# Attention units that end without TensorE transposes: softmax sums exchanged by transfers

## The chip, the cores and the metric

One Trainium2 chip, one of its cores. The metric is the device time of one execution in microseconds (us), the median of three runs. The kernel is written for one launch, and nothing is computed on the host.

## The reference

The kernel computes one transformer block with a conditioning vector `c`. A row `mod = silu(c) @ w_mod` gives six vectors of 512 (`sa, ca, ga, sb, cb, gb`). Then

```
h = layernorm(x) * (1 + ca) + sa
q, k, v = h @ wq, h @ wk, h @ wv      # 32 heads of 16 columns, one k and one v for all
p = softmax(q k^T / 4)                # 2048 x 2048 for each head
x = x + ga * ((p v, heads side by side) @ wo)
h = layernorm(x) * (1 + cb) + sb
x = x + gb * (relu(h @ w1) @ w2)      # w1: 512 x 1792, w2: 1792 x 512
```

`x` is 2048 x 512, everything is float32.

## The kernel before, in words

**Blocks and units.** The 2048 queries are eight blocks of 256 (`NB`, `TB`). A block has four units, one for each group of eight heads, so there are 32 units (`NU`). A unit holds 8 heads x 256 queries against 2048 keys, in 16 steps of 128 keys (`KT`).

**The main loop** (L837) takes two steps in a turn: 256 turns `c`, eight to a unit. TensorE's 128 x 128 array is used as two halves of 64 rows: a matmul on rows 0 to 63 and one on rows 64 to 127 run side by side, so the program hands out work to the halves in pairs. A turn issues, in the order of the two strings `PARTS` (L39):

- 8 score matmuls (L713, half `h` of each in letters `c` and `d`); ScalarE (ACT) takes the exponential of each into SBUF (L715);
- 8 matmuls for the maxima of the next unit's scores (L417, letters `a` and `b`); VectorE (DVE) reduces each of them (L419). There are three PSUM banks for scores (`ps_exp`) and three for maxima (`ps_max`);
- the products of the exponentials with v, 2 x 4 matmuls on column quarters of the array (L831, `ps_pv`), which end each half of a turn. v carries sixteen columns of ones, so each quarter of `ps_pv` holds 16 rows of sums of p v (numerators) and 16 equal rows of sums of p (denominators), for 2 heads x 256 queries along the free dimension: the quarter's rows 0 to 15 are numerators, its rows 16 to 31 denominators;
- one *portion* of other work, six matmuls or twelve short ones, each issued once for each half (L166, letters `l` and `u`, bank `ps_fill`): first the q projections of later blocks, and from turn 32 on the rest of the layer for the block before (`behind(b)`, L502). Where nothing is left, six dummy matmuls take the portion's place (L855).

**How a unit ends.** `normalise` (L718) copies `ps_pv` to SBUF (ACT, L723). In the next turn, at letter `t`, four 128 x 128 pieces of that copy are transposed on TensorE into a `ps_max` bank, in two halves (`on_half`, L162; a change of half within a bank is fenced by a nop at L159), so that queries lie on the partitions. DVE then takes the reciprocals of the denominators (L731, 128 x 16) and multiplies (L734, twice) into `on[b]`, queries by features.

**What is behind.** `behind(b)` starts at turn 32(b+1) and lasts 32 portions. Before the change these are: 1 portion carried over from block b-1, 4 of the output projection (`out_proj`), 7 of the second layer's second half for block b-1, 14 of the first layer (`dense1`, its weights `w1s` fetched again from DRAM, 512 KB a portion), and 6 of the 7 portions of the second layer for its own first 128 queries (`second(b, 0)`, L516); the seventh is carried over. The output projection needs `on[b]` with features on the partitions, so at the start `turned_too` (L507) queues two more turns of four transposes each (into one `ps_exp` and one `ps_max` bank), and `split_psum` (L239) takes each result apart into a rounded high part `oh` (ACT), a copy (ACT) and a low part `ol` (GpSimd, POOL). `add_psum` (L256) ends a chain of portions: ACT copies `ps_fill`, POOL adds.

**The tail.** After the last turn nothing else is left to overlap: the remaining portions run on the whole array (L149), the last unit is turned and normalised, and `behind_last` (L567) does block 7 alone: transposes of `on`, parts, 12 more matmuls of the second layer (`more(12)`), output projection, norm, both layers.

**Queues.** Every engine runs its instructions in program order, and nearly all transfers are issued by SyncE (SP) in program order too: an issue whose semaphore is not there yet holds all later ones. Tiles of a pool (`tag`, `bufs`) make the next writer wait for the last reader.

Of the kernel before, what the change touches and what calls it, by code (L numbers as in the profile page):

```python
# [19 lines left out]
P = 128  # L20
# [35 lines left out]
def build(tc, nc, cst, sb, ps, dr, x, wq, wk, wv, wo, w1, w2, c, w_mod, out):  # L56
# [72 lines left out]
    wkv = sb.tile([P, 512], F32, name="wkv", tag="on", bufs=1)  # L129
# [372 lines left out]
    def behind(b):  # L502
# [20 lines left out]
        x1, oo = open_block(b)  # L523
        for k2 in range(DC // 2):
            turned_too(on[b], oo, k2, (ps_exp, ps_max)[k2])
        yield from carried.pop() if carried else [[]]
# [191 lines left out]
    def normalise(u, pvt):  # L718
        b, g = divmod(u, NG)
        if g == 0:  # L720
            on[b] = sb.tile([P, TT, D], F32, name="on", tag="on", bufs=1)
        pvs = sb.tile([P, 512], F32, name="pvs", tag="pvs", bufs=1)
        nc.scalar.activation(pvs, pvt, AF.Copy)  # L723

        def turn():
            pt = ps_max()

            def end():
                pv = pt.rearrange("p (h t c n) -> p h t c n", h=2, t=TT, c=4)
                rc = sb.tile([P, 4, 4], F32, name="rc", tag="rc", bufs=2)  # L730
                nc.vector.reciprocal(  # L731
                    rc, pt.rearrange("p (j c n) -> p j c n", j=4, c=4)[:, :, :, DH])
                for t in range(TT):
                    nc.vector.tensor_tensor(  # L734
                        on[b][:, t, g * P:(g + 1) * P].rearrange(
                            "p (c h n) -> p h c n", c=4, h=2),
                        pv[:, :, t, :, 0:DH],
                        rc.rearrange("p (h t) c -> p h t c", h=2)[:, :, t, :, None]
                        .to_broadcast([P, 2, 4, DH]), op=OP.mult)

            return [("turn", pt[:, j * P:(j + 1) * P], pvs[:, j * P:(j + 1) * P])
                    for j in range(4)], end

        return turn
# [70 lines left out]
    norm = pvt = None  # L815
# [9 lines left out]
    def values(s):  # L825
        nonlocal norm, pvt
# [6 lines left out]
        if kt == KT - 1:  # L833
            norm = normalise(u, pvt)
        next(todo, None)

    for c in range(NU * KT // 2):  # L837
# [9 lines left out]
        if norm is not None:  # L847
            turns.insert(0, norm)
            norm = None
# [63 lines left out]
```

## Time and profile before

| what | before |
|---|---|
| three runs, us | 1836.94, 1827.8, 1823.17 (median 1827.8) |
| the profiled execution, us | 1838.22 |
| its span, first to last instruction, us | 1836.4 |
| mean granted TensorE clock over the span | 0.965 |
| the same in the loop, 373 to 572 us | 1.00 |
| instructions | 34397 |

The prediction uses the page (busy times, chain), the view by windows (busy time of each engine within a stretch), the timeline, the groups of instructions, the tile view and the waits. `PEld` is TensorE's weight load, `PEq` its sequencer, `SPq` the issuing of a transfer. A row such as `96.98 7.40 DMA qdr<-qq` in the chain gives start and length in us.

### The profile page before, as it was taken

The page shows a single profiled execution, that of the slowest core. Times are in us where ns is not written, and L with a number is a line of the kernel's source. Part 1 is how long each engine was busy: PE and PEld are TensorE (multiplying, and loading weights), DVE is VectorE, ACT ScalarE, POOL GpSimd, SP SyncE. Part 2 cuts the span into 40 slices and gives each one's busy share as a digit, 9 for nine tenths or more (in the row PEclk, how much of TensorE's full clock was granted, in tenths as well). Part 3 has the DMA queues.
Part 4 walks back from the last instruction along what each step waited for, and adds up shares of the span by engine and source line. Part 5 has one row for each costly group of instructions (what it writes and reads, how often), then busy time and mean ns, then how long its engine had stood idle before and what let it go on. Part 6 is the DMA issues. An engine that isn't in the chain of part 4 may idle for free.

```text
span 1836.4 us, 34397 instructions
## 1 busy us (share of the span) xinstructions
PE 1783.1 (97%) x13485; PEld 957.6 (52%) x13485; DVE 1394.8 (76%) x2408; ACT 1239.7 (68%) x2378; POOL 315.5 (17%) x386
## 2 busy tenths in 40 slices
PE   7988999999999999999999999999999999999987
PEld 5323444444654456545654465445654565446566
DVE  4655777888888888888888888888888888888021
ACT  3326666776777677777777777767777777777820
POOL 5555100012010211031101201121103110120000
PEclk9557999999999999999999999999999999999999
DMA  7653122101310123011310131012201131013123
GB/s 240 203 160 89 57 74 62 56 10 44 100 47 27 33 76 88 13 47 49 94 33 17 41 110 45 27 33 76 87 13 47 53 90 33 18 45 96 36 81 115
DMA packets 64704, 122.36 MB, mean 67 GB/s; under 512 B 8224, under 2 KB 30752, under 8 KB 64544
## 3 DMA queue, kind: packets, MB, share of 16 engines
q1 hardware_dynamic: 61904, 117.99, 20.8%
q8 instruction: 109, 1.79, 0.4%
q10 hardware_dynamic: 2640, 2.17, 0.4%
q14 instruction: 51, 0.42, 0.1%
HBM read 95.49 MB, written 24.12 MB: 65 GB/s over the span
## 4 chain that ended last, share of the span: by engine, by line
PE 86%; DVE 6%; ACT 2%; DMA 2%; POOL 2%; issue 1%; SPq 0%; POOLq 0%; DVEq 0%; ACTq 0%
PE ps_pv L831 27%; PE ps_exp L713 18%; PE ps_fill L166 17%; PE ps_max L417 17%; DVE pm L419 4%; PE ps_exp L149 1%; PE ps_max L162 1%; PE ps_exp L306 1%; PE ps_max L149 1%; ACT stg L243 1%; DMA w1s<-w1dr 1%; DVE st L201 1%; POOL w2r L234 1%; PE ps_exp L162 1%; DMA wmod<-in_w_mod_dram 1%
## 5 line engine op out<-in xcount | busy, mean ns | idle before, releaser
L419 DVE TENSOR_REDUCE pm<-ps_max 128x1 f32<-128x512 f32 x2048 | 1298.4, 684 | 250.5 <-PE ps_max L417 208.7
L715 ACT ACTIVATE pe<-ps_exp 128x512 f32<-128x512 f32 x2048 | 1082.9, 604 | 382.1 <-PE ps_fill L166 155.8
L417 PE MATMUL ps_max<-kp,qp 48*128 48x512 f32 x2048 | 840.4, 455 | 9.1 <-DVE pm L419 4.5
L713 PE MATMUL ps_exp<-qp,kp 50*128 50x512 f32 x2048 | 728.6, 415 | 10.6 <-DMA raw<-in_B_w_dram 7.7
L831 PE MATMUL ps_pv<-pe,vt 128*32 128x512 f32 x4096 | 546.3, 605 | 0.0
L417 PEld LDWEIGHTS ps_max<-kp,qp 48*128 48x128 f32 x2048 | 371.9, 190 | 253.1 <-DVE pm L419 201.5
L713 PEld LDWEIGHTS ps_exp<-qp,kp 50*128 50x128 f32 x2048 | 360.5, 186 | 272.8 <-ACT pe L715 172.0
L166 PE MATMUL ps_fill<-w2r,r 64*128 64x512 f32 x1068 | 319.5, 411 | 0.0
L166 PE MATMUL ps_fill<-hh,w1s 64*128 64x256 f32 x1568 | 244.7, 286 | 0.0
L166 PEld LDWEIGHTS ps_fill<-hh,w1s 64*128 64x128 f32 x1568 | 215.7, 186 | 7.7 <-PEq L159 3.4
L166 PEld LDWEIGHTS ps_fill<-w2r,r 64*128 64x128 f32 x1068 | 184.5, 185 | 10.8 <-PEq L159 4.2
L831 PEld LDWEIGHTS ps_pv<-pe,vt 128*32 128x32 f32 x4096 | 80.6, 108 | 165.8 <-issue 146.2
L247 POOL TENSOR_TENSOR r<-stg,r 128x512 fp32r<-128x512 f32 x49 | 62.8, 1281 | 551.2 <-ACT r L246 551.2
L166 PE MATMUL ps_fill<-hl,w1s 64*128 64x256 f32 x784 | 131.8, 285 | 0.0
L166 PE MATMUL ps_fill<-hT,wq 64*128 64x512 f32 x208 | 116.5, 648 | 0.0
L166 PEld LDWEIGHTS ps_fill<-hl,w1s 64*128 64x128 f32 x784 | 108.3, 186 | 0.0
L731 DVE RECIPROCAL rc<-ps_max 128x16 f32<-128x16 f32 x32 | 8.3, 258 | 82.3 <-PE ps_max L146 43.4
L247 POOL TENSOR_TENSOR ol<-stg,oh 128x512 fp32r<-128x512 f32 x14 | 17.6, 1283 | 272.4 <-ACT stg L243 272.4
L166 PE MATMUL ps_fill<-kp 64*128 64x512 f32 x180 | 53.7, 410 | 0.0
L259 POOL TENSOR_TENSOR x<-stg,x 128x512 f32<-128x512 f32 x14 | 18.0, 1288 | 152.2 <-ACT stg L258 152.2
L247 POOL TENSOR_TENSOR qq<-stg,qq 128x512 fp32r<-128x512 f32 x14 | 18.1, 1290 | 147.2 <-ACT qq L246 147.2
L243 ACT ACTIVATE stg<-ps_fill 128x512 f32<-128x512 f32 x63 | 38.4, 609 | 5.2 <-PE ps_fill L166 5.0
(149 smaller groups left out, 1060.9 us busy)
## 6 DMA issues: line engine op xcount, KB each, us to landing
w1s<-w1dr SPq DMA_DIRECT2D x112, 512.0 KB
qdr<-qq SPq DMA_DIRECT2D x48, 256.0 KB
qp<-qdr SPq DMA_DIRECT2D x128, 96.0 KB
raw<-in_B_w_dram SPq DMA_DIRECT2D x28, 256.0 KB
w1dr<-w1s SPq DMA_DIRECT2D x14, 512.0 KB
wmod<-in_w_mod_dram SPq DMA_DIRECT2D x4, 1024.0 KB
qp<-ms SPq DMA_DIRECT2D x256, 2.0 KB
x<-in_A_x_dram SPq DMA_DIRECT2D x8, 512.0 KB
```

The costliest lines, as they stand in the source:

```text
L149: nc.tensor.matmul(pt, w, a, start=start, stop=stop)
L162: ins = nc.tensor.transpose(pt[:, r], d[2][r], idn[r, r])
L166: ins = nc.tensor.matmul(pt, w[r], a[r], start=start and h == 1, stop=stop and h == 0)
L201: nc.vector.bn_stats(st, src)
L234: (eng or nc.gpsimd).tensor_tensor(lo, src, hi.bitcast(F32), op=OP.subtract)
L243: nc.scalar.activation(stg, pt, func, **kw)
L247: nc.gpsimd.tensor_tensor(lo, stg, hi.bitcast(F32), op=OP.subtract)
L417: nc.tensor.matmul(pt, qps[u][i][r, j * P:(j + 1) * P], kp[r, kb * 512:(kb + 1) * 512], start=True, stop=True)
L419: nc.vector.tensor_reduce(pms[u][:, (i * 2 + hf) * 4 + j, kb:kb + 1], pt, axis=AX.X, op=OP.max)
L713: nc.tensor.matmul(pt, kp[r, kt * P:(kt + 1) * P], qps[u][ct // 2][r], start=True, stop=True)
L715: nc.scalar.activation(pe, pt, AF.Exp)
L831: nc.tensor.matmul(pvt[i * 32:(i + 1) * 32], vt[:, kt], pes.pop((s, i)), start=(kt == 0), stop=(kt == KT - 1))
```

## The change

**Units.** `normalise` makes no turn any more. POOL copies the first 256 columns of the copied sums to a tile `num`; four transfers bring the numerators of the other 256 columns into the 16 rows of each quarter that held denominators, so that `num` holds features on the partitions and 256 queries along the free dimension, in the order in which the output projection wants them. For the denominators, four transfers write one row of each quarter to DRAM (`sums`, 8 x 256); one reads them back as 128 x 16 (`rc`); DVE takes the 128 x 16 reciprocals; one transfer writes them to DRAM (`recs`), and one reads them back with each row spread over 16 partitions (`den`, 128 x 256). POOL multiplies `num` by `den` into `on[b]`, now features by queries. The two closing steps are held in a list `ends`: `back` (reciprocal and two transfers) is issued at the end of the second turn after the unit, the product at the end of the third. The last unit goes another way: its denominators are exchanged like its numerators (four transfers into `den`), DVE takes all 128 x 256 reciprocals, POOL multiplies.

**Blocks.** `on[b]` needs no transposes: the eight in `behind` and the eight of `behind_last` are gone, and `split` (L232) makes `oh` and `ol` from SBUF, one ACT and one POOL instruction each. In `behind_last` `oh` and `ol` are made from SBUF too. `behind(b)` starts with three portions carried over instead of one, and runs four of `second(b, 0)` instead of six at its end; the parts are queued after the second of the three. Everything between stands two turns later in the block. Block 0 has three empty portions instead of one.

```diff
@@ build @@
-    wkv = sb.tile([P, 512], F32, name="wkv", tag="on", bufs=1)
+    wkv = sb.tile([P, 512], F32, name="wkv", tag="pvs", bufs=1)
@@ behind @@
         x1, oo = open_block(b)
+        rest = carried.pop() if carried else iter([[]] * 3)
+        yield next(rest)
+        yield next(rest)
         for k2 in range(DC // 2):
-            turned_too(on[b], oo, k2, (ps_exp, ps_max)[k2])
-        yield from carried.pop() if carried else [[]]
+            put_off.append(partial(split, flat(oo[0], k2), flat(oo[1], k2), flat(on[b], k2)))
+        yield from rest
...
-        yield from itertools.islice(first_half, 6)
+        yield from itertools.islice(first_half, 4)
         carried.append(first_half)
@@ behind_last @@
         for k2 in range(DC // 2):
-            pt = ps_exp()
-            run_all(turned(on[b], k2, pt))
-            parts(flat(oo[0], k2), flat(oo[1], k2), pt)
+            parts(flat(oo[0], k2), flat(oo[1], k2), flat(on[b], k2))
@@ normalise @@
-            on[b] = sb.tile([P, TT, D], F32, name="on", tag="on", bufs=1)
+            on[b] = sb.tile([P, DC, TB], F32, name="on", tag="on", bufs=1)
         pvs = sb.tile([P, 512], F32, name="pvs", tag="pvs", bufs=1)
         nc.scalar.activation(pvs, pvt, AF.Copy)
-        def turn():
-            pt = ps_max()
...
+        num, den = [sb.tile([P, TB], F32, name=n, tag=n, bufs=1) for n in ("num", "den")]
+        nc.gpsimd.tensor_copy(num, pvs[:, 0:TB])
+        for c in range(4):
+            nc.sync.dma_start(num[c * 32 + DH:(c + 1) * 32], pvs[c * 32:c * 32 + DH, TB:])
+        if u == NU - 1:
+            nc.gpsimd.tensor_copy(den, pvs[:, TB:])
+            for c in range(4):
+                nc.sync.dma_start(den[c * 32:c * 32 + DH], pvs[c * 32 + DH:(c + 1) * 32, 0:TB])
+            return [partial(nc.vector.reciprocal, den, den), partial(
+                nc.gpsimd.tensor_tensor, on[b][:, g], num, den, op=OP.mult)]
+        sums, recs = [dr.tile([8, TB], F32, name=n, tag=n, bufs=2) for n in ("sums", "recs")]
+        for c in range(4):
+            nc.sync.dma_start(
+                sums[c * 2:c * 2 + 2],
+                pvs[c * 32 + DH:c * 32 + DH + 1].rearrange("p (h n) -> p h n", h=2))
+        rc = sb.tile([P, DH], F32, name="rc", tag="rc", bufs=2)
+        nc.sync.dma_start(rc, sums.rearrange("j (a n) -> (j a) n", n=DH))
+        def back():
+            nc.vector.reciprocal(rc, rc)
+            nc.sync.dma_start(recs.rearrange("j (a n) -> (j a) n", n=DH), rc)
+            nc.sync.dma_start(den, recs[:, None].to_broadcast([8, DH, TB]))
+        return [back, partial(nc.gpsimd.tensor_tensor, on[b][:, g], num, den, op=OP.mult)]
@@ values @@
         if kt == KT - 1:
-            norm = normalise(u, pvt)
+            ends.extend((s // 2 + 2 + n, end) for n, end in enumerate(normalise(u, pvt)))
@@ main loop @@
-        if norm is not None:
-            turns.insert(0, norm)
-            norm = None
...
             values(s + part)
+        if ends and ends[0][0] <= c:
+            ends.pop(0)[1]()
...
     in_turn(put_off)
-    turned_now, end = norm()
-    for d in turned_now:
-        on_all(d)
-    end()
+    for _, end in ends:
+        end()
     behind_last(NB - 1)
```

How this moves instructions shows at three places. The first is TensorE at the start of a unit in the loop (turn 64 of the program before), from inside the first half of the turn to inside the second.

```order
L417 MATMUL ps_max<-kp,qp 128x512
L166 MATMUL ps_fill<-w2r,r_4840 128x512
L162 MATMUL ps_max<-idn,pvs 128x64 x4
L713 MATMUL ps_exp<-qp,kp 128x512
L166 MATMUL ps_fill<-w2r,r_4840 128x512
L417 MATMUL ps_max<-kp,qp 128x512
L166 MATMUL ps_fill<-w2r,r_4841 128x512
L831 MATMUL ps_pv<-pe,vt 32x512 x4
L162 MATMUL ps_max<-idn,pvs 128x64 x4
L417 MATMUL ps_max<-kp,qp 128x512
```

The same place now (L714 is the scores, L841 the products with v):

```order
L417 MATMUL ps_max<-kp,qp 128x512
L166 MATMUL ps_fill<-w2r,r_5013 128x512
L714 MATMUL ps_exp<-qp,kp 128x512
L166 MATMUL ps_fill<-w2r,r_5013 128x512
L417 MATMUL ps_max<-kp,qp 128x512
L166 MATMUL ps_fill<-w2r,r_5014 128x512
L841 MATMUL ps_pv<-pe,vt 32x512 x4
L417 MATMUL ps_max<-kp,qp 128x512
```

Both groups of four half transposes are gone, and with them the `ps_max` bank that they held from the one to the other.

The second place is SP's queue over two units of one block in the program now: the end of a unit (`num`, `sums`, `rc`), weights of the first layer, the second half of the exchange (`recs`, `den`), the next unit's queries.

```order
L443 DMA w1s<-w1dr_115 128x1024
L732 DMA num<-pvs 16x256 x4
L743 DMA sums<-pvs 1x512 x4
L747 DMA rc<-sums 128x16
L443 DMA w1s<-w1dr_116 128x1024
L443 DMA w1s<-w1dr_117 128x1024
L751 DMA recs<-rc 128x16
L752 DMA den<-recs 128x1x256
L443 DMA w1s<-w1dr_118 128x1024
L373 DMA qp<-qdr_0_130 48x2x256 x4
```

Before, this queue held only the loads of `w1s`, `qp` and `x`, the rows of maxima `qp<-ms`, and the output; eleven transfers a unit are new, and two of them (`rc`, `den`) wait on SP for one issued just before them.

The third place is DVE at the tail, from the last unit to the first addition of the output projection, before:

```order
L731 RECIPROCAL rc<-ps_max 128x16
L734 TENSOR_TENSOR on<-ps_max,rc 128x2x4x16 x2
L595 TENSOR_TENSOR ol<-ps_exp,oh 128x512 x2
```

and now:

```order
L893 RECIPROCAL den<-den 128x256
L598 TENSOR_TENSOR ol<-on,oh 128x512 x2
```

DVE has one reciprocal of 256 elements a partition where it had one of 16 and two products; the product has gone to POOL (L893 there too), ahead of the last part that ACT makes.

More of the change, by code (lines that the diff above doesn't have):

```diff
@@ L720, in normalise @@
         if g == 0:
-            on[b] = sb.tile([P, TT, D], F32, name="on", tag="on", bufs=1)
+            on[b] = sb.tile([P, DC, TB], F32, name="on", tag="on", bufs=1)
         pvs = sb.tile([P, 512], F32, name="pvs", tag="pvs", bufs=1)
         nc.scalar.activation(pvs, pvt, AF.Copy)
-        def turn():
-            pt = ps_max()
[L728 to L742, printed above, removed]
@@ L744, in normalise @@
-        return turn
+        num, den = [sb.tile([P, TB], F32, name=n, tag=n, bufs=1) for n in ("num", "den")]
[8 more added lines that the diff above has]
+                nc.gpsimd.tensor_tensor, on[b][:, g], num, den, op=OP.mult)]
@@ L814, in build @@
     portion = next(others)
-    norm = pvt = None
+    pvt, ends = None, []
     def advance():
@@ L825, in values @@
     def values(s):
-        nonlocal norm, pvt
+        nonlocal pvt
         u, kt = divmod(s, KT)
```

## The prediction

> **What bounds the kernel now.** I read the page's busy times and the chain first: TensorE (PE) carries 86% of the chain.
>
> ```profile
> PE 1783.1 (97%) x13485; PEld 957.6 (52%) x13485; DVE 1394.8 (76%) x2408; ACT 1239.7 (68%) x2378; POOL 315.5 (17%) x386
> PE 86%; DVE 6%; ACT 2%; DMA 2%; POOL 2%; issue 1%; SPq 0%; POOLq 0%; DVEq 0%; ACTq 0%
> ```
>
> An average doesn't say what a transpose costs, so the next view is the loop, cut into stretches from one group of sums (L831, the end of half a turn) to the next but one. Each stretch is one turn long. The columns are the stretch, its length, then busy time of PE, PEld, DVE, ACT, POOL, the granted clock, DMA share and GB/s.
>
> ```profile
> 373.00:572.00 199.00, 196.91 (x1651) 108.23 (x1648) 169.92 (x288) 147.14 (x286) 25.83 (x32) 1.00 0.16 47
> 586.42:592.19 5.77, 5.77 (x46) 2.89 (x44) 5.06 (x10) 4.13 (x9) 0.00 (x0) 1.00 0.36 114
> 716.43:722.72 6.29, 6.29 (x65) 4.01 (x68) 5.54 (x9) 5.51 (x12) 1.28 (x1) 1.00 0.38 119
> 722.72:729.16 6.44, 6.44 (x66) 3.97 (x68) 5.23 (x12) 4.34 (x9) 0.00 (x0) 1.00 0.15 33
> 572.08:579.05 6.97, 6.97 (x59) 3.62 (x57) 5.74 (x12) 4.28 (x9) 0.00 (x0) 1.00 0.00 0
> 579.05:586.42 7.37, 7.12 (x54) 3.36 (x53) 4.78 (x9) 6.25 (x13) 3.81 (x3) 1.00 0.01 2
> ```
>
> An ordinary turn (second row) lasts 5.77 us, PE busy all of it, DVE 5.06, ACT 4.13. PE sets the pace, and DVE has 0.7 us a turn to spare. The third row holds the first half of a unit's transposes, 0.52 us longer; the fourth the second half, 0.67 longer. The last two lie at the start of a block: 0.53 above the unit's 6.44, then 1.60 above an ordinary turn. These stretches are what the change can shorten.
>
> **What the unit's transposes cost.**
>
> ```profile
> L162 PE MATMUL ps_max<-idn,pvs x248: 214/222/273, 210.9 to 1715.5; 64*128 64x64 f32 x124
> PEld ps_max L162 <- PEq L159: 52.0, 62, 0.8
> 720.88 2.57 DVE L419 TENSOR_REDUCE pm<-ps_max 128x1 f32<-128x512 f32 x4 [0.38 <-PE ps_exp L713]
> 724.15 0.26 DVE L731 RECIPROCAL rc<-ps_max 128x16 f32<-128x16 f32 x1 [0.70 <-PE ps_max L417]
> 724.44 0.49 DVE L734 TENSOR_TENSOR on<-ps_max,rc 128x128 f32<-128x128 f32 x2
> 724.85 2.48 DVE L419 TENSOR_REDUCE pm<-ps_max 128x1 f32<-128x512 f32 x4
> 730.63 2.60 DVE L419 TENSOR_REDUCE pm<-ps_max 128x1 f32<-128x512 f32 x4 [0.35 <-PE ps_max L417]
> ```
>
> 248 half transposes in 31 units are eight a unit. They stand on one half of the array with nothing paired on the other, behind a nop for which the weight load waits 0.84 us (second row, 52.0 over 62, which counts the turned maxima too), and DVE's three instructions stand ahead of the four reduces of that half turn: without them these would start at 720.88 + 2.57 + the usual idle 0.35 = 723.8, not at 724.85. Both go. The unit's price is 0.52 + 0.67 = 1.19 us. What stays is the copy of the sums (ACT, L723), 0.6 us ahead of the next exponentials, hidden until now beside the transposes; I leave 0.1 for it, 1.09 saved. With 30 units whose turns have maxima: 32.7. In the 31st, no maxima are left:
>
> ```profile
> 1711.33 1.06 PE L831 MATMUL ps_pv<-pe,vt 128*32 128x512 f32 x8
> 1717.14 1.07 PE L831 MATMUL ps_pv<-pe,vt 128*32 128x512 f32 x8
> 1722.60 1.07 PE L831 MATMUL ps_pv<-pe,vt 128*32 128x512 f32 x8
> ```
>
> Two turns: 5.81 with both halves of the transposes, 5.46 without, so 0.35. Sum 33.
>
> **Blocks.** The start of a block costs 0.53 + 1.60 = 2.13 above the unit's share, seven times.
>
> ```profile
> 580.54 0.60 ACT L242 ACTIVATE oh<-ps_exp 128x512 fp32r<-128x512 f32 x1 [1.07 <-PE ps_exp L162]
> 581.70 2.52 POOL L247 TENSOR_TENSOR ol<-stg,oh 128x512 fp32r<-128x512 f32 x2 [38.09 <-ACT stg L243]
> 582.66 0.49 PE L417 MATMUL ps_max<-kp,qp 48*128 48x512 f32 x1 [0.25 <-ACT stg L243]
> ```
>
> ACT's four instructions on the two results hold the scores up (PE idles 0.25). Now they are two from SBUF, 1.2 us of ACT; turn 722.72 to 729.16 shows ACT at 4.34, so two more fit. I take 2.0 of the 2.13: 14. The norm of the second layer moves two turns later, its second transposes onto a turn that already turns the maxima; DVE's part of it costs the same wherever it stands. I count nothing, with 0.3 a block either way.
>
> **The exchange.** It has two dates. DVE reaches the reciprocal `rc` behind the eighth reduce group of two turns: t0 being the unit's last sums (720.3, since ACT copies them at 720.44 below), that group ends at 733.23, 12.9 after t0, and 1.2 earlier without the transposes: 11.7. At the start of a block ACT wants `on[b]` in the third turn, behind two exponentials: 3 x 5.77 + 0.5 + 2 x 0.5 = 18.8.
>
> ```profile
> 720.44 0.60 ACT L723 ACTIVATE pvs<-ps_pv 128x512 f32<-128x512 f32 x1 [0.25 <-PE ps_pv L831]
> L132 POOL COPY wkv<-wkv 128x64 f32<-128x64 f32 x8 | 1.6, 244 | 3.9 <-DMA wkv<-in_A_wk_dram 3.7 <-DMA wkv<-in_A_wv_dram 0.2
> L475 POOL TENSOR_TENSOR xn<-xn,cbr 128x512 f32<-128x512 f32 x15 | 19.2, 1280 | 1.2
> 585.96 0.36 SPq L521 DMA_DIRECT2D out_dram<-ot  x1
> 606.37 4.97 SPq L393 DMA_DIRECT2D qp<-ms  x8
> SPq L909 <- DMA out_dram<-ot: 1.7, 1, 1.7
> 96.98 7.40 DMA qdr<-qq
> 1786.81 4.92 DMA w1s<-w1dr
> ```
>
> ACT's copy is there at 0.75, POOL's copy of 256 columns (between 0.24 for 64 and 0.64, half of 512) at 1.2. SP then issues eight small transfers. One issue costs 0.36 (a plain row) to 0.62 (eight small rows in 4.97): 2.9 to 5.0 us. I take 0.6, the small rows being the kin. For the landing after the issue no row shows so small a transfer: 1.7 us is the last 256 KB to DRAM, alone; the dear end is three of 256 KB behind each other, 7.40 less 1.8 of issue, 5.6. Nothing excludes less than 1.7, which changes no date. I take 1.7, since these are 2 to 128 KB. Then `rc` is there at 1.2 + 5.0 + 1.7 + 0.6 + 1.7 = 10.2, 1.5 before DVE wants it. Reciprocal until 12.0, `recs` 14.3, `den` 16.6, product (0.65) 17.3, 1.5 before ACT wants it. So the likeliest exchange is hidden, though barely: with a landing of 2.5 both dates are just met.
>
> What waits if not: behind `rc` on DVE all reduces, hence the `ps_max` banks and PE; behind `num`, `rc` and `den` on SP the loads of `w1s` and `qp`, used two turns (11.5 us) later and 4.92 long, so a delay of 4 is harmless. Two unit ends in a block have a load of `w1s` issued just ahead of the small transfers. Sharing the rings with it may cost them a microsecond; I set 4 us in all for such waits (14 ends x 0.3), bounds 0 and 17. POOL gains a copy and a product a unit, 1.1 us of an engine busy 17%.
>
> The Trainium skill, DMA: Bandwidth & Descriptors, section on the anatomy of one DMA, puts the fixed part of a transfer at about 2.0 us, written for transfers issued by GpSimd, nearly all of it the receipt of the write, heaviest in HBM. By it the estimate for `rc` would be 10.8 instead of 10.2, still early, and the sum the same; the 1.7 above is nearer to this queue. It raises the chance of the second rival.
>
> **The tail.**
>
> ```profile
> 1756.37 3.04 PE L149 MATMUL ps_fill<-w2r,r 128*128 128x512 f32 x12
> 1759.25 0.60 PE L146 MATMUL ps_max<-idn,pvs 128*128 128x128 f32 x4
> 1759.69 1.37 PE L146 MATMUL ps_exp<-idn,on 128*128 128x128 f32 x8
> 1760.81 3.01 PE L149 MATMUL ps_fill<-w2r,r 128*128 128x512 f32 x12
> 1763.66 1.10 PE L149 MATMUL ps_exp<-woh,oh 128*128 128x512 f32 x4
> L175 DVE RECIPROCAL sg<-sg 128x4 f32<-128x4 f32 x1 | 0.2, 178 | 0.0
> L731 DVE RECIPROCAL rc<-ps_max 128x16 f32<-128x16 f32 x32 | 8.3, 258 | 82.3 <-PE ps_max L146 43.4 <-PE ps_max L417 22.8 <-PE ps_max L162 16.2
> ```
>
> The output projection began 7.29 after the loop's end, its third matmul, the first that needs the last units, at 7.76. Now 24 + 12 matmuls at 0.24 come first: 8.6. But the last unit, from the loop's end: `num` copied 1.2, eight issues until 6.2, landed 7.9, reciprocal of 256 elements (178 to 258 ns over 12 elements is 6.7 ns an element, 1.86 us) 9.8, product 10.4, ACT's part 11.0. The third matmul moves from 7.76 to 11.0: 3.3 us later (1.3 with no wait at all, 7.2 with landings of 5.6).
>
> **Sum.** 33 + 14 - 4 - 3.3 = 39.7, say 40, against the profiled span of 1836.4: 1796. That execution took 1838.22, the three runs 1823.17 to 1836.94; the median, 1827.8, becomes **1788**.
>
> **Rivals.**
>
> *The transposes are in the shadow of something else.* PE's busy time may hide slack, and DVE at 170 of 199 is close behind; then only what the turns without maxima show is won: 31 x 0.35 + 7 x 0.65 - 3.3 = 12, 1816. For it speaks that a part of the 0.67 is DVE's; against it that DVE's work goes too, and that DVE idles 0.35 to 0.38 before each group of reduces. Chance 0.12. The Trainium skill, Perfetto Trace Analysis, on identifying the most-contended engine, says that matmul busy time is a poor measure and weight-load time a better one; that is 52% here. By that rule TensorE has room, and this rival would be right; the gapless stretches above speak for PE all the same.
>
> *The reciprocals come late (slower).* `rc` takes the place of the transposes as what DVE waits for, 31 times. Two landings stand in a row ahead of it, so each us of landing above 2.45 costs 2 us a unit, 62 in all. From a landing of 3.1 on (0.65 x 62 = 40, the gain), the change is slower; at 3.5 it gives 1788 + 65 = 1853, at the dear end of 5.6 some 1983. For it speaks that the slack is 1.5 us; against it the 1.7. Chance 0.10.
>
> *Only the block starts wait.* The 512 KB of `x` stand between `rc` and `recs` on SP there, and a load of that size took 4.92 above. If it makes `recs` or `den` land 4 us late, of which 1.5 are slack, ACT waits 2.5 seven times: 17, so 1805. Against it: issued at about 9, it should have drained when `recs` is issued at 12. Chance 0.10.
>
> **Chances.** Forecast 0.68. A measurement of this kernel tells about 1% (18 us) from nothing: faster holds the forecast and nearly all of the third rival, 0.77; within 1% the first rival and a remnant, 0.13; slower 0.10. The range: no waits and the cheap tail give 33 + 15 - 1.3, 1781, less 7 for the spread of the runs: 1774. Upwards it takes in the third rival and the first: 1816.
>
> **What would show it.** Right: turns at unit starts near 5.8 to 5.9 (two stretches of 11.7 instead of 12.7); the first turns of a block near 5.8; DVE not idle before L750; ACT not idle before its parts of `on`; the output projection's third matmul some 11 us after the last sums. Wrong: idle time of DVE before L750 ended by `rc<-sums` (late reciprocals); idle time of ACT or POOL at the block's third turn ended by `den<-recs`; or unit starts that stay above 6.1 with PE busy throughout, which would mean that the transposes weren't what made them long.

## The result and the profile after

| what | before | after |
|---|---|---|
| median of four runs beside each other, us | 1832.18 | 1773.16 |
| their lowest and highest, us | 1823.17, 1836.94 | 1772.68, 1776.23 |
| profiled span, us | 1836.4 | 1771.3 |
| from the first instruction to the sums that end the first half of the second turn, us | 163.98 | 149.96 |
| the loop: 254 turns from there to the sums that end the first half of the last turn, us | 1588.80 | 1536.02 |
| from there to the end, us | 83.62 | 85.32 |

The ratio is 0.9687, 95% interval 0.9642 to 0.9732: faster by 3.1%. The forecast was 1788 with a range from 1774 to 1816. The direction is right, and the gain is larger than forecast, 59 us against 40: the time lies 1 us below the range. The profiled executions differ by 65.1 us, and the three stretches of the table hold -14.0, -52.8 and +1.7 of it. Two executions among the runs of this document, 5317.33 us of the kernel before and 5252.67 of the one with earlier closing steps, took almost three times as long as all others and are left out of every median.

The first thing to read is whether all of this belongs to the change. The view by windows, cut at the same places, has these two rows for the kernel before (stretch, its length, busy time of PE, PEld, DVE, ACT, POOL with counts, granted clock, DMA share, GB/s):

```profile
163.98:1752.78 1588.80, 1574.10 (x12705) 839.31 (x12704) 1291.88 (x2185) 1177.02 (x2273) 222.47 (x257) 1.00 0.17 52
0.00:163.98 163.98, 140.16 (x409) 61.92 (x409) 83.85 (x172) 54.12 (x92) 88.47 (x126) 0.63 0.57 183
```

and these for the changed kernel:

```profile
149.96:1685.98 1536.02, 1526.95 (x12345) 816.60 (x12345) 1274.69 (x2123) 1165.36 (x2259) 257.70 (x319) 1.00 0.20 59
0.00:149.96 149.96, 123.31 (x409) 53.86 (x410) 84.44 (x172) 54.45 (x92) 88.70 (x126) 0.72 0.62 200
```

Ahead of the loop TensorE does the same 409 matmuls in both, as the change touches nothing there that it issues. It does them at a granted clock of 0.63 in the one and 0.72 in the other, and the second is 14 us shorter. In the loop the clock is 1.00 in both, so the loop can be compared with no such reservation: 52.8 us. The last experiment shows that the start differs from run to run of one and the same kernel; the loop lengths below leave it out.

The page's busy times and its chain by engine, after:

```profile
PE 1720.1 (97%) x13125; PEld 927.0 (52%) x13125; DVE 1379.0 (78%) x2344; ACT 1228.3 (69%) x2364; POOL 352.8 (20%) x451
PE 88%; DVE 4%; DMA 3%; ACT 2%; POOL 2%; issue 1%; SPq 0%; POOLq 0%; DVEq 0%; ACTq 0%
```

PE is busy 63 us less. Of these, 47 are in the loop, and 17 lie ahead of it, where the work is the same and the clock is not. It still carries the chain, 88% of it; DMA's share rises by one point only. The turns of the loop, after: an ordinary turn, the two turns of a unit's start, then from a block's start its first two turns and its ninth:

```profile
552.46:558.25 5.79, 5.79 (x47) 2.88 (x45) 5.23 (x10) 4.13 (x9) 0.00 (x0) 1.00 0.33 90
685.29:691.15 5.86, 5.86 (x58) 3.73 (x56) 5.13 (x9) 5.11 (x11) 1.68 (x2) 1.00 0.30 110
691.15:696.94 5.79, 5.79 (x58) 3.68 (x56) 4.99 (x9) 4.65 (x10) 0.00 (x0) 1.00 0.12 22
546.68:552.46 5.78, 5.78 (x47) 2.89 (x45) 4.93 (x9) 4.14 (x9) 0.00 (x0) 1.00 0.09 19
594.14:600.76 6.62, 6.03 (x46) 2.94 (x44) 5.91 (x13) 4.88 (x10) 0.95 (x5) 1.00 0.06 12
```

(The first row is at once the block's second turn, so it stands once.) The unit's start has 5.86 and 5.79 where it had 6.29 and 6.44. A whole unit of eight turns away from the block starts goes from 48.16 to 47.12. The block's first two turns are 5.78 and 5.79 where they were 6.97 and 7.37.

The exchange is read in the timeline, here at a block's start (start, length, engine, line, work; in brackets the idle time before and what ended it):

```profile
544.88 0.60 ACT L726 ACTIVATE pvs<-ps_pv 128x512 f32<-128x512 f32 x1 [0.29 <-PE ps_pv L841]
546.04 2.45 SPq L732 DMA_DIRECT2D num<-pvs  x4
548.53 1.32 SPq L743 DMA_DIRECT2D sums<-pvs  x4
550.90 0.34 SPq L747 DMA_DIRECT2D rc<-sums  x1
...
556.49 0.24 DVE L750 RECIPROCAL rc<-rc 128x16 f32<-128x16 f32 x1
556.76 0.33 SPq L751 DMA_DIRECT2D recs<-rc  x1
558.18 0.66 SPq L752 DMA_DIRECT2D den<-recs  x1
...
561.45 0.73 POOL L883 TENSOR_TENSOR on<-num,den 128x256 f32<-128x256 f32 x1 [15.44 <-PE ps_exp L714]
563.67 1.15 ACT L233 ACTIVATE oh<-on 128x512 fp32r<-128x512 f32 x2
```

SP holds an issue back until what it reads has landed, so the gaps between its rows are landings: from the end of the `sums` issues (549.85) to `rc` 1.05 us, from the end of `recs` (557.09) to `den` 1.09. DVE's reciprocal and ACT's parts have no idle time in front. POOL does wait: over the whole run it idles 185.2 us, in 20 waits, for `den`, at the third turn of some blocks too, which the prediction had named as a sign of being wrong. But no instruction waited in the loop for the product that POOL makes of it, and a unit with no exchange at all (below) is as long. In the loop's last stretch, where no reduces are left to stand in front, DVE does wait, and that one wait in the view of waits gives the landing of `rc`:

```profile
DVE rc L750 <- DMA rc<-sums: 20.6, 1, 20.6
```

```profile
1651.89 0.34 SPq L747 DMA_DIRECT2D rc<-sums  x1
1653.56 0.25 DVE L750 RECIPROCAL rc<-rc 128x16 f32<-128x16 f32 x1 [20.56 <-DMA rc<-sums]
```

1653.56 - 1652.23 = 1.33 us. At the tail, the changed kernel's timeline (the 24 and 12 matmuls of L149 are the remaining portions; the output projection's third matmul follows on 1700.81):

```profile
1689.56 5.78 PE L149 MATMUL ps_fill<-w2r,r 128*128 128x512 f32 x24
1697.22 1.75 DVE L893 RECIPROCAL den<-den 128x256 f32<-128x256 f32 x1 [43.41 <-DMA den<-pvs]
1700.81 0.73 PE L149 MATMUL ps_exp<-woh,oh 128*128 128x512 f32 x2 [1.24 <-ACT oh L594]
```

### The profile page after: what moved, and what is told of

Its sections match the earlier page's. It is cut to its first block, busy times and chain, and to the rows that moved or that the text cites. A ratio compares the mean times of both kernels' runs of the same rounds, so it can differ in the third digit from the quotient of the medians.

```text
span 1771.3 us, 34183 instructions
## 1 busy us (share of the span) xinstructions
PE 1720.1 (97%) x13125; PEld 927.0 (52%) x13125; DVE 1379.0 (78%) x2344; ACT 1228.3 (69%) x2364; POOL 352.8 (20%) x451
## 4 chain that ended last, share of the span: by engine, by line
PE 88%; DVE 4%; DMA 3%; ACT 2%; POOL 2%; issue 1%; SPq 0%; POOLq 0%; DVEq 0%; ACTq 0%
PE ps_pv L841 29%; PE ps_exp L714 20%; PE ps_fill L166 17%; PE ps_max L417 17%; DVE pm L419 3%; PE ps_exp L149 1%; PE ps_max L149 1%; DMA w1s<-w1dr 1%; DMA wmod<-in_w_mod_dram 1%; ACT hh L242 0%; DVE st L201 0%; POOL w2r L234 0%; ACT stg L243 0%; PE ps_exp L162 0%; DMA qdr<-qq 0%
## 5 line engine op out<-in xcount | busy, mean ns | idle before, releaser
L417 PE MATMUL ps_max<-kp,qp 48*128 48x512 f32 x2048 | 817.8, 446 | 7.2 <-DVE pm L419 4.7
L714 PE MATMUL ps_exp<-qp,kp 50*128 50x512 f32 x2048 | 725.5, 414 | 10.6 <-ACT pe L716 7.8
L841 PE MATMUL ps_pv<-pe,vt 128*32 128x512 f32 x4096 | 546.3, 605 | 0.0
L417 PEld LDWEIGHTS ps_max<-kp,qp 48*128 48x128 f32 x2048 | 368.1, 187 | 268.7 <-DVE pm L419 230.7
L714 PEld LDWEIGHTS ps_exp<-qp,kp 50*128 50x128 f32 x2048 | 360.0, 185 | 276.8 <-ACT pe L716 177.5
L166 PE MATMUL ps_fill<-w2r,r 64*128 64x512 f32 x1044 | 306.4, 407 | 0.0
L166 PEld LDWEIGHTS ps_fill<-w2r,r 64*128 64x128 f32 x1044 | 180.7, 185 | 7.7 <-PEq L159 2.5
L841 PEld LDWEIGHTS ps_pv<-pe,vt 128*32 128x32 f32 x4096 | 80.6, 108 | 163.2 <-issue 141.8
L166 PE MATMUL ps_fill<-hl,w1s 64*128 64x256 f32 x784 | 128.2, 282 | 0.0
L883 POOL TENSOR_TENSOR on<-num,den 128x256 f32<-128x256 f32 x31 | 22.8, 735 | 237.6 <-DMA den<-recs 185.2
L730 POOL COPY num<-pvs 128x256 f32<-128x256 f32 x32 | 12.8, 399 | 237.4 <-ACT pvs L726 237.4
L166 PE MATMUL ps_fill<-kp 64*128 64x512 f32 x204 | 59.4, 405 | 0.0
L247 POOL TENSOR_TENSOR hl<-stg,hh 128x512 fp32r<-128x512 f32 x14 | 18.1, 1290 | 111.2 <-ACT stg L243 111.2
```

What stands on the lines that cost most here:

```text
L166: ins = nc.tensor.matmul(pt, w[r], a[r], start=start and h == 1, stop=stop and h == 0)
L247: nc.gpsimd.tensor_tensor(lo, stg, hi.bitcast(F32), op=OP.subtract)
L417: nc.tensor.matmul(pt, qps[u][i][r, j * P:(j + 1) * P], kp[r, kb * 512:(kb + 1) * 512], start=True, stop=True)
L714: nc.tensor.matmul(pt, kp[r, kt * P:(kt + 1) * P], qps[u][ct // 2][r], start=True, stop=True)
L730: nc.gpsimd.tensor_copy(num, pvs[:, 0:TB])
L841: nc.tensor.matmul(pvt[i * 32:(i + 1) * 32], vt[:, kt], pes.pop((s, i)), start=(kt == 0), stop=(kt == KT - 1))
```

## The experiments

The theory: on TensorE's path stood the units' transposes (with DVE's three instructions), the eight transposes at each block's start, and, beside them, the order of the carried portions; the exchange costs nothing as long as its two dates are met. The rivals: the transposes lay in the shadow of other work and the gain has another source (the portions, or a start that the change makes faster). Each measured ratio is to the kernel before. "Loop" is that stretch of the table above; it is 1588.80 before and 1536.02 after. The whole time carries the chance of the start, 14 us and more, so the small parts are read from the loop.

### The portions alone

The kernel before, with three carried portions, all transposes kept:

```diff
@@ behind @@
+        rest = carried.pop() if carried else iter([[]] * 3)
+        yield next(rest)
+        yield next(rest)
         for k2 in range(DC // 2):
             turned_too(on[b], oo, k2, (ps_exp, ps_max)[k2])
-        yield from carried.pop() if carried else [[]]
+        yield from rest
...
-        yield from itertools.islice(first_half, 6)
+        yield from itertools.islice(first_half, 4)
```

> Kernel before with only the three carried portions (the transposes of on stay and are queued after the second of them). Theory (moving the norm two turns takes DVE's work away from the turns with the turned maxima and gives about 1 us a block): turns 5 and 7 of a block shrink by 0.5 and 0.6 us, its second unit keeps its sum, the loop is some 7 us shorter, the tail 2.8 us longer, in all 3 to 5 us faster than before. Rival (the move is neutral and the extra gain of the change came from elsewhere): the loop as before, in all 2 to 3 us slower.

Measured: 1824.59, ratio 0.9959 (0.9931 to 0.9987); loop 1580.02, 8.8 less; tail 2.4 longer. The prediction had this part at nothing. Its windows are read turn against turn. The kernel before, the fifth and seventh turn of a block (the norm's work on DVE), the ninth, the eleventh (second transposes) and the thirteenth (turned maxima):

```profile
597.97:604.81 6.84, 6.32 (x47) 2.96 (x45) 6.44 (x13) 4.87 (x10) 0.00 (x0) 1.00 0.01 2
610.81:617.43 6.62, 6.03 (x47) 2.96 (x45) 6.15 (x14) 4.88 (x10) 0.95 (x5) 1.00 0.53 176
623.69:630.13 6.44, 6.44 (x50) 3.03 (x48) 5.22 (x12) 3.84 (x8) 2.91 (x3) 1.00 0.00 0
636.42:643.48 7.06, 6.87 (x54) 3.42 (x52) 5.21 (x9) 5.20 (x11) 1.30 (x1) 1.00 0.00 0
650.07:656.36 6.29, 6.20 (x54) 3.51 (x52) 5.78 (x11) 5.12 (x11) 1.29 (x1) 1.00 0.03 12
```

and the same turns of the kernel with the portions moved:

```profile
581.41:587.69 6.28, 6.19 (x48) 2.97 (x46) 5.78 (x11) 4.63 (x10) 0.00 (x0) 1.00 0.12 44
593.70:599.70 6.00, 6.00 (x46) 2.94 (x44) 5.62 (x11) 4.36 (x10) 0.00 (x0) 1.00 0.47 180
605.98:613.14 7.16, 6.68 (x50) 3.09 (x49) 6.29 (x16) 4.72 (x10) 0.95 (x5) 1.00 0.00 1
618.91:624.69 5.78, 5.78 (x47) 2.89 (x45) 5.07 (x10) 4.13 (x9) 3.44 (x4) 1.00 0.00 0
630.94:638.03 7.09, 6.89 (x56) 3.52 (x54) 5.47 (x10) 5.24 (x11) 1.30 (x1) 1.00 0.01 2
```

Per row: -0.56, -0.62, +0.72, -1.28, +0.80. The first piece of the norm stood before on a turn in which DVE was already at 5.78 with the turned maxima, and brought it to 6.44 of 6.84, 0.56 longer. Two turns later it costs 0.23: the seventh turn is 6.00, and 5.77 with neither piece on it (in the run with one turn of shift, below). The second piece cost 0.85 over that 5.77, and costs 0.72 in the ninth turn. Together the norm gives some 0.5 a block.

The second transposes give more. They take three turns, the tenth to the twelfth before (6.29, 7.06, 6.59), and the turned maxima then make the next two 6.29 and 6.02. Now they are the twelfth to the fourteenth (6.25, 7.09, 6.58), and the last two of these hold the turned maxima too. They are no longer than they were without them, so the 0.5 and 0.2 of the turned maxima are saved, and the tenth and eleventh turn are ordinary: some 0.8 a block. Why the two don't add up there was not tried. Over the block's first sixteen turns it is 102.38 against 101.13, 1.25 less, times seven 8.8.

### The portions moved by one turn

The kernel before, with two carried portions:

```diff
@@ behind @@
+        rest = carried.pop() if carried else iter([[]] * 2)
+        yield next(rest)
         for k2 in range(DC // 2):
             turned_too(on[b], oo, k2, (ps_exp, ps_max)[k2])
-        yield from carried.pop() if carried else [[]]
+        yield from rest
...
-        yield from itertools.islice(first_half, 6)
+        yield from itertools.islice(first_half, 5)
```

> Kernel before with two portions carried over instead of one (three in the run with the shift alone), transposes of on queued after the first. Theory (0.7 of the 1.2 us that the shift by two turns won come from the second layer's transposes sharing turn 13 with the turned maxima, the rest from the norm's sums leaving turn 4): here those transposes stand in turns 11 and 12, beside nothing, and the sums fall on turn 5 with DVE's copies of the maxima, so the block's first two units lose 0 to 0.5 us, not 1.2; against before the loop is 0 to 3.5 us shorter, the tail 1.2 longer. Rival (any shift off turns 4 and 6 wins it): the block loses 1.2 us again.

Measured: 1828.46, ratio 0.9987 (0.9955 to 1.0019), no difference that can be told by the time; loop 1586.17, 2.6 less, 0.37 a block. The block's eighth turn, to which the norm's second piece comes, and its twelfth and thirteenth in the windows of this kernel:

```profile
612.81:620.04 7.23, 6.31 (x51) 3.18 (x49) 6.76 (x15) 5.28 (x11) 1.38 (x7) 1.00 0.19 54
638.52:645.61 7.09, 6.89 (x55) 3.44 (x53) 5.23 (x9) 5.21 (x11) 1.29 (x1) 1.00 0.00 0
645.61:652.71 7.10, 6.82 (x52) 3.15 (x50) 5.46 (x10) 5.32 (x11) 1.29 (x1) 1.00 0.01 2
```

In the eighth turn the second piece meets a unit's end, DVE is at 6.76, and the turn lasts 7.23 where it lasts 6.26 in the kernel before: 0.96 for a piece that cost 0.85. The first piece, in the sixth turn, costs 0.12 (6.12 against 6.00). That leaves the norm's move a gain of some 0.3. The second transposes stand in the eleventh to the thirteenth turn, and only their last part meets the turned maxima, in the thirteenth. There the two do add up: 7.10, where the transposes' part alone took 6.59 and the maxima alone 6.29, each over an ordinary 5.78. So their move gives nothing here, where two turns gave 0.8. What a shift is worth is a matter of which turns the pieces meet.

### The units' transposes left out

```diff
@@ normalise @@
         nc.scalar.activation(pvs, pvt, AF.Copy)
-        def turn():
-            pt = ps_max()
...
-        return turn
+        for t in range(TT):
+            nc.gpsimd.tensor_copy(on[b][:, t, g * P:(g + 1) * P], pvs[:, t * P:(t + 1) * P])
@@ main loop @@
-        if norm is not None:
-            turns.insert(0, norm)
-            norm = None
```

> Kernel before without the units' transposes, reciprocals and products: two copies on GpSimd fill on instead, so the division by the sums is left out. Theory (the turn is on the path of TensorE and DVE): every unit start loses 1.0 to 1.2 us, 31 to 36 us in all. Rival (the turn lies in the shadow of something else): 0.35 us a unit, 11 us in all.

Measured: 1793.84, ratio 0.9802 (0.9749 to 0.9854); loop 1556.67, 32.1 less. The two turns of a unit's start in this kernel:

```profile
698.06:703.94 5.88, 5.88 (x59) 3.74 (x57) 5.15 (x9) 5.12 (x11) 1.80 (x3) 1.00 0.32 108
703.94:709.74 5.80, 5.80 (x59) 3.66 (x57) 4.96 (x9) 4.62 (x10) 0.00 (x0) 1.00 0.21 53
```

They are the changed kernel's 5.86 and 5.79 within 0.02, and a whole unit away from the block starts is 47.13 against 47.12 there. So the units' transposes, with DVE's instructions behind them, were on the path for 32 us, and the exchange that took their place in the changed kernel costs such a unit nothing: this kernel has no exchange at all. The first rival of the prediction (shadow, 12 us) has fallen.

### TensorE's part of it alone

The transposes stay, DVE's reciprocal and products are left out:

```diff
@@ normalise @@
+        for t in range(TT):
+            nc.gpsimd.tensor_copy(on[b][:, t, g * P:(g + 1) * P], pvs[:, t * P:(t + 1) * P])
...
-            def end():
...
             return [("turn", pt[:, j * P:(j + 1) * P], pvs[:, j * P:(j + 1) * P])
-                    for j in range(4)], end
+                    for j in range(4)], lambda: None
```

> Kernel before with the units' transposes on TensorE, but DVE's reciprocal and two products left out (on is filled by copies on GpSimd, so the division is left out). Splits the unit's 1.19 us: theory, TensorE's part about 0.85 (0.5 in the first half, 0.35 in the second), DVE's 0.3, so 9 to 10 us faster than before. Rival (the price is DVE's alone): 1.0 us a unit or more comes off, over 30 us.

Measured: 1815.12, ratio 0.9933 (0.9899 to 0.9966); loop 1573.11, 15.7 less than before and 16.4 more than without the transposes. Its turns at a unit's start:

```profile
697.05:703.34 6.29, 6.29 (x63) 4.01 (x61) 5.54 (x9) 5.52 (x12) 1.81 (x3) 1.00 0.37 118
703.34:709.28 5.94, 5.94 (x63) 3.90 (x61) 4.66 (x9) 4.22 (x9) 0.00 (x0) 1.00 0.15 32
```

Against 6.29 and 6.44 before, DVE's instructions are 0.50 of the second turn; against 5.88 and 5.80 without transposes, TensorE's are 0.41 and 0.14. Half and half, where TensorE's share had been expected to be nearly three times DVE's. DVE was busy 5.23 of that turn's 6.44 and set 0.50 of it all the same. (That its three instructions delay the reduces behind them, and so the banks that PE wants back, fits the rows that the prediction quotes, but is argued.)

### The transposes of `on` left out

```diff
@@ behind @@
         for k2 in range(DC // 2):
-            turned_too(on[b], oo, k2, (ps_exp, ps_max)[k2])
+            put_off.append(partial(split, flat(oo[0], k2), flat(oo[1], k2), on[b][:, k2]))
```

> Kernel before with the transposes of on in the loop left out; its parts are made from on as it lies, so the output projection sums over the wrong index. Everything else stands where it was. Theory: turns 0 and 1 of a block lose 0.5 and 1.6 us, seven times, 15 us; all else in the block as before. Rival (ACT's parts, not TensorE, made these turns long): they keep 0.5 us or more of it.

Measured: 1817.51, ratio 0.9925 (0.9893 to 0.9956); loop 1574.46, 14.3 less, 2.05 a block. The block's first two turns, 6.97 and 7.37 before:

```profile
569.29:575.71 6.42, 6.42 (x51) 3.05 (x49) 5.22 (x12) 3.84 (x8) 0.00 (x0) 1.00 0.00 0
575.71:581.53 5.82, 5.82 (x46) 2.88 (x44) 5.06 (x10) 5.63 (x12) 3.83 (x3) 1.00 0.00 0
```

ACT is busy 5.63 of the second one's 5.82, with the two parts in it, and the turn is as good as ordinary: two parts from SBUF fit into a turn, as the prediction had it. So it was TensorE's transposes, with ACT's four instructions on their results, that made these turns long. The run takes out both at once and doesn't split them.

### The closing steps a turn earlier

The changed kernel, with the reciprocals at the end of the first turn after the unit instead of the second, and the product behind the second:

```diff
@@ values @@
-            ends.extend((s // 2 + 2 + n, end) for n, end in enumerate(normalise(u, pvt)))
+            ends.extend((s // 2 + 1 + n, end) for n, end in enumerate(normalise(u, pvt)))
```

> Changed kernel with both closing steps one turn earlier (reciprocal at the end of the first turn after the unit, product at the end of the second). By the changed trace the row of sums is back about 7.9 us after the unit's last sums, and DVE would reach the reciprocal at 5.9. Theory (what DVE waits for passes to TensorE once its slack of 0.7 us is used up): 1.3 to 2 us a unit, 40 to 60 us slower than the changed kernel. Rival (three PSUM banks and the slack take it up): under 10 us.

Measured: 1830.07, the median of nine runs, ratio 1.0014 (0.9974 to 1.0053): no gain that can be told by the time. Loop 1587.94, 51.9 more than in the changed kernel. From its waits, from its timeline at the start of a unit, and from its windows the second turn of a unit's start, 5.79 in the changed kernel:

```profile
DVE rc L750 <- DMA rc<-sums: 68.9, 31, 20.6
```

```profile
517.61 0.60 ACT L726 ACTIVATE pvs<-ps_pv 128x512 f32<-128x512 f32 x1 [0.24 <-PE ps_pv L841]
525.17 0.25 DVE L750 RECIPROCAL rc<-rc 128x16 f32<-128x16 f32 x1 [1.61 <-DMA rc<-sums]
526.02 0.49 PE L417 MATMUL ps_max<-kp,qp 48*128 48x512 f32 x1 [0.96 <-DVE pm L419]
```

```profile
720.45:727.51 7.06, 6.06 (x58) 3.74 (x57) 4.98 (x9) 5.88 (x12) 0.92 (x1) 1.00 0.26 70
```

`rc` is there 7.6 us after ACT began its copy, DVE asked for it 1.6 earlier, and PE then idles 0.96 for a bank that DVE gives back late. Without the last wait of 20.6, which no reduces follow, (68.9 - 20.6) / 30 = 1.6 a unit. This is the mechanism of the prediction's second rival. Its price in a turn at full clock is 7.06 - 5.79 = 1.27 for 1.6 of wait.

In 31 units that makes some 39 of the 51.9 us. Most of the rest goes with the granted clock: in six stretches of 50 us in this loop it is 0.97 and in one 0.93, while in the changed kernel's loop it is 1.00 throughout. Six times 0.03 and once 0.07 of 50 us make 12.5 us (an estimate from these figures). Whether the new waits of PE bring the lower clock with them was not tried. One turn of distance separates the changed kernel from all of this.

### What limits it next

Three things were changed at once in the changed kernel, so their sum is measured and not each: the norm's last statistics one turn later, beside the normed rows that need them; at the tail `den` copied ahead of `num` and its transfers issued by ACT; the tail's second layer in another PSUM bank.

```diff
@@ behind @@
             ln_sums(mv, 1, x1[:, 1])
-            stats = ln_stats(mv, TT, False)
             yield
-            normed(x1, xn, range(TT), *stats, nc.gpsimd)
+            normed(x1, xn, range(TT), *ln_stats(mv, TT, False), nc.gpsimd)
...
@@ behind_last @@
         def second(t):
-            pt = ps_fill()
+            pt = ps_exp()
...
@@ normalise @@
+        if u == NU - 1:
+            nc.gpsimd.tensor_copy(den, pvs[:, TB:])
+            for c in range(4):
+                nc.scalar.dma_start(den[c * 32:c * 32 + DH], pvs[c * 32 + DH:(c + 1) * 32, 0:TB])
         nc.gpsimd.tensor_copy(num, pvs[:, 0:TB])
```

> Changed kernel with three edits: the norm's statistics one turn after its second sums, the rest of the norm right behind them; at the tail the last unit's denominators copied first and their four transfers issued by ACT's queue; the second layer's last half in a score bank at the tail. Theory: turn 8 of a block loses 0.6 us of its 0.83 and turn 9 gains at most 0.1, so 3 to 4 us in the loop; the output projection's third matmul comes 1.4 to 2 us earlier after the loop's end. In all 5 us faster than the changed kernel at the same clock. Rival (GpSimd's norm then comes late for the transposes, or the statistics cost the same wherever they stand): the loop stays as it is.

Measured: 1781.12, ratio 0.9718 (0.9683 to 0.9754); loop 1532.13, 3.9 less than the changed kernel's, tail 83.29, 2.0 less. The block's ninth turn, 6.62 in the changed kernel, and the third matmul of the tail:

```profile
605.82:611.82 6.00, 6.00 (x47) 2.96 (x45) 5.39 (x10) 4.37 (x10) 0.21 (x1) 1.00 0.07 14
```

```profile
1707.64 0.73 PE L149 MATMUL ps_exp<-woh,oh 128*128 128x512 f32 x2 [0.67 <-ACT oh L593]
1710.47 0.69 DVE L606 TENSOR_TENSOR x<-ps_exp,x 128x512 f32<-128x512 f32 x1 [2.15 <-DMA x<-in_A_x_dram]
```

The turn is 0.62 shorter (0.56 a block in the loop: 3.9 / 7), and the tenth, to which the statistics moved, stays at 5.79: they cost some 0.6 behind the sums and nothing a turn later. The matmul comes 1.6 earlier after the loop's end (1707.64 - 1697.99 = 9.65), and behind it stands a new wait of 2.15 for the load of `x`. To compare this kernel with the changed one by its time, the start has to be equal, and that is the next run's subject.

### The changed kernel again

Nothing is edited.

> The changed kernel once more, for the clock at the start. Theory (the granted clock of the first 150 us varies from run to run whatever the kernel, and moves the time by up to 16 us): its runs spread from 1773 to some 1788, with the clock, and the median gain over before is near 50 us. Rival (the change brings a faster start itself): all runs within 5 us of 1773, before spread as it was, gain 59.

Measured: 1780.03 over six runs, ratio 0.9731 (0.9689 to 0.9772); loop 1536.28, within 0.3 of the first. Its stretch ahead of the loop, and that of the kernel just above, each from its windows:

```profile
0.00:149.09 149.09, 118.11 (x409) 54.48 (x409) 83.58 (x172) 54.43 (x92) 88.51 (x126) 0.78 0.62 202
```

```profile
0.00:162.28 162.28, 139.08 (x409) 61.72 (x409) 83.86 (x172) 54.04 (x92) 88.37 (x126) 0.63 0.57 185
```

The six runs fall into two groups by the mean granted clock of the run: 1772.12, 1773.82 and 1775.11 at 0.973 to 0.980; 1784.95, 1785.58 and 1788.1 at 0.963 to 0.965. Of the 22 runs of the kernel before beside them, nine are at 0.973 to 0.980 with a median of 1822.69 and eleven at 0.964 to 0.966 with 1836.28; two lie between, and the 25 runs beside the first four experiments fill the whole stretch from 1821.66 to 1839.45. So the start takes between 149 and 164 us by chance, with the change and without it, and the rival that the change makes the start faster has fallen. At equal clocks the change brings 1822.69 - 1773.82 = 48.9 and 1836.28 - 1785.58 = 50.7: some 50 us, 2.7%. The first measurement's 59 holds 50 of the change; its four runs of the changed kernel were all at 0.973 to 0.975. The kernel above, at 0.963 to 0.965 (median of five 1781.22), is 4.4 faster than the changed kernel at the same clock; its one run at 0.974, 1769.81, is 5.3 faster than the one there, 1775.11.

| loop, us | against before |
|---|---|
| the changed kernel | -52.8 |
| units' transposes left out | -32.1 |
| of these DVE's instructions alone | -15.7 |
| transposes of `on` left out | -14.3 |
| portions moved by two turns | -8.8 |
| portions moved by one turn | -2.6 |
| changed, closing steps a turn earlier (some 12 us more without its lower clock) | -0.9 |

The three parts (32.1, 14.3, 8.8) make 55.2, the changed kernel has 52.8. Most of the difference lies in the block's second unit: 49.89 where 50.77 less the parts' 1.10 and 0.08 would be 49.59, 0.3 in each of seven blocks. Which instruction sets it there was not tried.

## Why the prediction was right, and where not

**Units, 33: right, with a wrong split.** 32.1 measured. The price of 1.19 was read from whole stretches (6.29 and 6.44 against 5.77), so it didn't matter who made them long. The prediction named TensorE's transposes and DVE's three instructions and gave no split. Its row of DVE had the reduces 1.05 late for the three (724.85 against 723.8); taken out alone they gave 0.50 of the stretch, half of the whole. What the stretches lose is 0.41 + 0.64 = 1.05 by the kernel without transposes, and I had saved 1.09.

**Blocks, 14: right.** 14.3.

**The moved norm and second transposes, 0 with 0.3 a block either way: the step that failed.** They gave 8.8, 1.25 a block. The prediction saw that the second transposes come onto a turn that already turns the maxima, and put that at nothing. But beside the transposes the turned maxima cost nothing more: some 0.8 a block. And it said that DVE's part "costs the same wherever it stands". The norm's first piece cost 0.56 in the fifth turn and costs 0.23 in the seventh, the second 0.85 and 0.72: some 0.5 a block. The rows to ask were there: before, the fifth turn had DVE at 6.44 of 6.84, the thirteenth was long already, at 6.29. A step that is moved has to be priced in both turns, the one it leaves and the one it comes to.

**Waits of the exchange, -4: nothing.** `rc` landed at 550.90 + 0.34 + 1.33 = 552.57 (by the landing of 1.33 measured in the loop's last stretch), and the unit's last sums ended at 544.88 - 0.29 = 544.59: 8.0 us, not 10.2. Two terms were too dear: the eight issues took 3.81 (546.04 to 549.85), not 5.0, since a row of one partition costs 0.33 to issue and only the `num` rows the 0.6 that I took for all; and the landings are 1.05 and 1.33, not 1.7. DVE took `rc` 11.9 after the sums, forecast 11.7, so the slack was 3.9, forecast 1.5. The ACT date: asked for at 563.67, 19.1 after the sums (forecast 18.8), `on` ready at 562.18. The load of 512 KB of `x`, the third rival's cause, delayed neither. On this the Trainium skill, DMA: Bandwidth & Descriptors, in the section on the anatomy of one DMA, gives a fixed part of about 2.0 us, for transfers issued by GpSimd; SP's transfers of 2 to 8 KB here took half to two thirds of that after the issue.

**The tail, -3.3: right in the step, not in the end.** The third matmul came 1700.81 - 1689.56 = 11.25 after the start of the remaining portions, which the prediction calls the loop's end; forecast 11.0, before 7.76. Yet the end came only 1.7 later. The windows from the second normed rows to the second layer, before and after, and the transposes of these rows in the two chains tell where the rest went:

```profile
1777.72:1812.43 34.71, 25.66 (x176) 23.53 (x177) 5.54 (x8) 4.78 (x8) 2.52 (x2) 0.90 0.56 174
1714.38:1747.56 33.18, 25.05 (x176) 22.89 (x177) 5.44 (x8) 4.77 (x8) 2.52 (x2) 0.95 0.56 183
```

```profile
1780.38 1.77 PE ps_exp L146 x7
1717.04 0.56 PE ps_exp L146 x3
```

The stretch is 1.5 less, and 1.2 of that are the transposes, on the chain for 1.77 us before and for 0.56 after. So most of the difference between 3.5 and 1.7 lies in transposes that the change doesn't touch. The granted clock over the stretch was 0.90 before and 0.95 after; that it made the difference fits, but isn't shown. The tail of the kernel without the transposes of `on`, which is the tail before unedited, took 1822.7 - 1737.84 = 84.86 us against 83.62, so a difference of 1.2 there can be chance.

**The base.** The sum was made against a profiled execution whose start took 164 us and laid on a median over both kinds of start. At equal starts the forecast of 40 stands against 50: 9 of the moved portions, 4 of waits that did not come, 2 of the tail, less 1 of the units and some 2 to 3 by which the parts are less together (52.8 - 1.7 = 51). That the time lies just under the range, 15 below the forecast, is 10 of gain, and for the other 5 that the four runs all had the shorter start, while 1827.8 lay between the two.

**The rivals.** Shadow: fallen (32.1). The Trainium skill, Perfetto Trace Analysis, on identifying the most-contended engine, calls matmul busy time a poor measure of how close TensorE is to its limit and weight-load time a better one; that was 52% before and is 52% after, and yet taking TensorE's work out of the loop gave time at once. Here the measurement decides for the stretches in which PE had no gap, with the reservation that DVE set half of the units' share. Late reciprocals: did not happen, but the mechanism is real and a turn away, at 1.27 us in the turn shown. Block starts: no wait.

## What to carry to other kernels

Price a change by whole stretches of the loop against an ordinary one, and then price every step that merely moves, in the turn it leaves and in the turn it enters: here two turns of shift were worth 9 us and one turn 2.6. A chain of small transfers through DRAM, some 8 us here from the sums to the landing, is free where its consumer stands in a queue whose date can be read; asked for one turn too early, it cost some 39 of the 53 us that the loop had gained. Compare parts of the trace at equal granted clock before giving the whole difference to the change.

## What the runs showed of the hardware

- The same 409 matmuls ahead of the loop took between 148.6 and 164.0 us in the ten profiled executions, at granted clocks from 0.78 down to 0.62. The times of one and the same kernel spread accordingly. No run here shows what decides it.
- In the loop with the closing steps a turn earlier, where PE idled about 1 us in the second turn of a unit, the granted clock was 0.93 to 0.97 in seven stretches of 50 us; in the changed kernel's loop, without that wait, it stayed at 1.00.
- Small transfers issued by SP: 0.33 us an issue for one row, 0.61 for 16 partitions of 1 KB, 0.66 for one that spreads each row over 16 partitions; landing 1.05 to 1.33 after the issue.
- Four half transposes twice a unit, with nothing paired on the other half of the array, made the two turns 0.55 us longer (0.41 and 0.14), and the 0.26 + 0.49 us of DVE behind them 0.50 more, though DVE was busy 5.23 of that turn's 6.44.
- Twelve half transposes over two turns (7.09 and 6.58) took no longer with the turned maxima in the same turns than without them (7.06 and 6.59); four in one turn with them did (7.10).
